# The product x·v and its fold into u on one engine, and another share of evictions, in a long convolution with two MLPs

## The chip, the cores and the metric

The kernel runs on one core of a Trainium2 chip. The metric is the device time of one execution in microseconds, taken as the median of several. A core has TensorE (matrix products), VectorE, ScalarE and GpSimd (elementwise work, each on its own instruction queue) and SP (here it only sends transfers). The trace calls them PE, DVE, ACT, POOL and SP; PEld is TensorE's loading of weights. ScalarE's queue sends transfers too.

## What is computed

A gated long convolution over 12480 positions and 128 channels, then two MLPs of width 2048 in a row:

```python
h_filt = (np.maximum(pos_emb @ w1, 0.0) @ w2) * np.exp(-0.01 * pos)[:, None]
u = x * v
y = irfft(rfft(u, n=2 * S) * rfft(h_filt, n=2 * S), n=2 * S)[:S]
a = x * y
a = np.square(np.maximum(a @ moe_w_in, 0.0)) @ moe_w_out
h = a @ moe2_w_in
out = (h / (1.0 + np.exp(-1.702 * h))) @ moe2_w_out
```

## The kernel before

The convolution is done as products with transform matrices: 12480 positions are laid out as 99 × 127 (with padding), so that a first transform works on 99 partitions and a second one, stage_s2, on the rest. Positions j and -j of the short side are folded into their sum and their difference. The stages follow one another: the filter's hidden layer (filter_stage), the first transform, the second transform with the spectral product and the first half of the inverse (stage_s2), and then one long loop (mlp) that does the last transform and both MLPs tile by tile.

The change lies in the first transform. It has 48 steps of s1_step: 16 over the filter's 64 features (source h, destination G), then 32 over the 128 channels of u (destination A), four columns in each. A step is eight matrix instructions of 99 × 198 (L280) into one of four PSUM banks of the pool cps, and an eviction of that bank, either on VectorE (L284 and L286) or on ScalarE (L288 to L290). Every third step is evicted by VectorE, `f // 4 % 3 == 2`.

u is made beside it, in 16 chunks of eight channels (class Inputs); each chunk serves two of the 32 later steps. load sends x and v of a chunk on SP's queue, in four transfers (L196, L197); chunks 0 to 4 have buffers of their own, the later ones share three (vp), so that load c waits until chunk c-3 has been folded. multiply forms x·v in place on GpSimd, in two halves (L207), and for the even chunks also the sum (even, L215); odd forms the difference on VectorE (L225), and for odd chunks the sum too. u itself has seven buffers, so chunk c needs that the steps of chunk c-7 have been multiplied.

The order is written out by hand (manual_schedule): what is issued first in the code stands first in its engine's queue. advance, called behind each step, issues one multiply, an odd where the step is in the set odds (after steps 1, 4, 6, 9, 11, 13, 16, 18, 21, 23, 25, 28, 30, 33, 35 and 37 of the 48), and then a load if buffers allow. Two more multiplies are issued beside the filter's last two groups. After steps 22, 26, 30 and 34 ScalarE's queue writes a quarter of G to DRAM (gd, L666); stage_s2 reads it back as Gs (load_h, L306), first after step 42. After step 41 the pool of x and v is closed, and w2b (L672) and five loads of matrices m (load_m, L299) are sent on SP in the room that it leaves.

Of the kernel before, what the change touches and what calls it, by code (L numbers as in the profile page):

```python
# [9 lines left out]
FP32 = mybir.dt.float32  # L10
# [4 lines left out]
ALU = mybir.AluOpType  # L15
# [8 lines left out]
N1, N2 = 99, 127  # L24
NT = N1 * N2
JC = N2 // 2
NJ = JC + 1
# [6 lines left out]
XC = 8  # L34
NXC = D // XC
# [5 lines left out]
JF = 8  # L41
# [50 lines left out]
def conv_mlp_kernel(ctx: ExitStack, tc: tile.TileContext, xc, xt, vc, pt, w1, w2,  # L92
                    moe_w_in, moe_w_out, moe2_w_in, moe2_w_out,
                    c_s1, c_s2, c_i2, c_win, out):
    nc = tc.nc
# [84 lines left out]
    class Inputs:  # L180


        def __init__(self, up, pool, first, early):
            self.up, self.pool, self.tiles, self.u = up, pool, {}, {}
            self.first, self.early = first, early
            self.loaded = self.done = self.odd_done = 0

        def load(self):
            c = self.loaded
            if c == NXC or c >= self.early and c - max(self.odd_done, self.early) == 3:  # L190
                return
            self.loaded += 1
            pool, bufs = (self.first, self.early) if c < self.early else (self.pool, 3)
            xs, vs = (pool.tile([N1, XC, 2, NJ], FP32, tag=n, name=n, bufs=bufs) for n in ("x", "v"))
            for r in (slice(0, ROWS), slice(ROWS, N1)):
                nc.sync.dma_start(out=xs[r], in_=xc[c, r])  # L196
                nc.sync.dma_start(out=vs[r], in_=vc[c, r])  # L197
            self.tiles[c] = xs, vs

        def multiply(self):  # L200
            c = self.done
            if c == self.loaded:
                return
            self.done += 1
            xs, vs = self.tiles[c]
            for i in range(0, XC, 4):
                nc.gpsimd.tensor_tensor(out=xs[:, i:i + 4], in0=xs[:, i:i + 4], in1=vs[:, i:i + 4],  # L207
                                        op=ALU.mult)
            self.u[c] = self.up.tile([N1, XC, 2 * NJ], FP32, tag="u", name="u", bufs=7)
            if c % 2 == 0:  # L210
                self.even(c, nc.gpsimd)

        def even(self, c, engine):
            xs, _ = self.tiles[c]
            engine.tensor_tensor(out=self.u[c][:, :, 0:NJ], in0=xs[:, :, 0], in1=xs[:, :, 1], op=ALU.add)  # L215

        def odd(self):
            c = self.odd_done
            if c == self.done:
                return  # L220
            self.odd_done += 1
            if c % 2:
                self.even(c, nc.vector)
            xs, _ = self.tiles.pop(c)
            nc.vector.tensor_tensor(out=self.u[c][:, :, NJ:2 * NJ], in0=xs[:, :, 0], in1=xs[:, :, 1],  # L225
                                    op=ALU.subtract)

    def filter_stage(fp, bank, h, inputs):

        HC = 4  # L230
        NC_ = NJ // HC
        bw1 = fp.tile([128, 128], FP32, name="bw1", bufs=1)
        warm = fp.tile([128, 1], FP32, name="warm", bufs=1)
        win = fp.tile([N1, 2, NJ], FP32, name="win", bufs=1)
        nc.vector.memset(warm, 0.0)
        p_t = {}

        def load_pos(c):
            p = fp.tile([128, HC, N1], FP32, tag="pos", name="pos", bufs=12)
            nc.sync.dma_start(out=p, in_=pt[:, c * HC:(c + 1) * HC, :])  # L240
            p_t[c] = p

        nc.scalar.dma_start(out=bw1, in_=w1)
        for c in range(12):
            load_pos(c)
        nc.scalar.dma_start(out=win, in_=c_win)
        nc.scalar.activation(out=warm, in_=warm, func=ACTF.Sigmoid)
        nc.scalar.dma_start(out=cs1, in_=c_s1)
        nc.vector.memset(sign[:, 0:1], 1.0)
        nc.vector.memset(sign[:, 1:2], -1.0)  # L250

        for j in range(0, NJ, JF):
            for c in range(j // HC + 12, min(j // HC + 12 + JF // HC, NC_)):
                load_pos(c)
            if j >= JF:
                inputs.load()
            ps = bank("hp")[:N1]
            for i in range(JF):
                nc.tensor.matmul(out=ps[:, i * 2 * F:(i + 1) * 2 * F],
                                 lhsT=p_t[(j + i) // HC][:, (j + i) % HC, :], rhs=bw1)  # L260
            r = fp.tile([N1, 2, F, JF], FP32, tag="r", name="r")
            for s in range(2):
                wb = win[:, s, j:j + JF].unsqueeze(1).to_broadcast([N1, F, JF])
                nc.vector.scalar_tensor_tensor(
                    out=r[:, s], in0=ps.rearrange("p (j s f) -> p s f j", j=JF, s=2)[:, s],
                    scalar=0.0, in1=wb, op0=ALU.max, op1=ALU.mult)
            last = j + JF == NJ
            (nc.vector if last else nc.gpsimd).tensor_tensor(
                out=h[:, :, j:j + JF], in0=r[:, 0], in1=r[:, 1], op=ALU.add)
            nc.vector.tensor_tensor(out=h[:, :, NJ + j:NJ + j + JF], in0=r[:, 0], in1=r[:, 1],  # L270
                                    op=ALU.subtract)
            if j >= NJ - 2 * JF:
                inputs.multiply()

    def s1_step(bank, src, d, dst, on_vector):

# [17 lines left out]
    def load_m(mp, p):  # L294
        if p >= NP:
            return
        n = min(2, N1 - 2 * p)
        m_t[p] = mp.tile([128, 2, 2, 128], FP32, tag="m", name="m", bufs=7)
        nc.sync.dma_start(out=m_t[p][:, 0:n], in_=c_s2[:, 2 * p:2 * p + n])  # L299
# [327 lines left out]
    with tc.manual_schedule():  # L627
# [4 lines left out]
        def bank(name):  # L632
            return cps.tile([128, 1024], FP32, tag="b", name=name)
# [1 line left out]
        G = sgs.enter_context(tc.tile_pool(name="G", bufs=1, side="right")).tile(  # L635
            [128, N1, 2, F], FP32, name="G")
        vp = vps.enter_context(tc.tile_pool(name="v", bufs=3, side="right"))
        odds = {-(-12 * c // 5) + 1 for c in range(NXC)}
        steps = [0]

        def advance():
            inputs.multiply()
            if steps[0] in odds:
                inputs.odd()
            inputs.load()
            steps[0] += 1

        with tc.tile_pool(name="h", bufs=1) as hp:
            h = hp.tile([N1, F, 2 * NJ], FP32, name="h")
            inputs = Inputs(up, vp, hp, 5)  # L650
            with tc.tile_pool(name="fil", bufs=2) as fp:
                filter_stage(fp, bank, h, inputs)
            for f in range(0, F, 4):
                s1_step(bank, h, f, G[:, :, :, f:f + 4], f // 4 % 3 == 2)
                advance()
            assert inputs.odd_done >= inputs.early
        with tc.tile_pool(name="A", bufs=1, reuse_waits="tile") as ap_, ExitStack() as mps:
            A = ap_.tile([128, N1, 2, D], FP32, name="A")
            for d in range(0, D, 4):
                s1_step(bank, inputs.u[d // XC], d % XC, A[:, :, :, d:d + 4], d // 4 % 3 == 2)  # L660
                if d // 4 < 25:
                    advance()
                if d // 4 in (6, 10, 14, 18):
                    q = 25 * (d // 16 - 1)
                    q = slice(q, min(q + 25, N1))
                    nc.scalar.dma_start(out=gd[:, q], in_=G[:, q].rearrange("p k c f -> p k (c f)"))  # L666
                if d // 4 == 25:
                    assert inputs.odd_done == NXC
                    vps.close()
                    mp = mps.enter_context(tc.tile_pool(name="mh", bufs=1, reuse_waits="tile"))  # L670
                    w2b = mp.tile([128, 2 * D], FP32, name="w2b")
                    nc.sync.dma_start(out=w2b, in_=w2)  # L672
                if d // 4 in (25, 26, 27, 28, 29):
                    load_m(mp, d // 4 - 25)
                if d // 4 in (26, 28):
                    load_h(mp, (d // 4 - 26) // 2)
            sgs.close()
            ups.close()
            w0 = ctx.enter_context(tc.tile_pool(name="w0", bufs=1, side="right", reuse_waits="tile"))
            split_weights(w0, 0)  # L680
            cp = ctx.enter_context(tc.tile_pool(name="cvt", bufs=1, side="right", reuse_waits="tile"))
            lp = ctx.enter_context(tc.tile_pool(name="lp", bufs=2, side="right", reuse_waits="tile"))
            nc.sync.dma_start(out=ci2, in_=c_i2)
            work = Weights([0, 4, 1, 5, 2, 6], 3, 7, 5, cp, [(44, 3), (46, 7)])
            hooks = {44: [lambda: load_x(lp, 0)]}
            with tc.tile_pool(name="s2", bufs=1, side="right", reuse_waits="tile") as sp:
                stage_s2(sp, mp, A, w2b, hooks, work)
# [91 lines left out]
```

## Time and profile before

| | us |
|---|---|
| median of three runs | 1455.44 (1452.51 to 1455.81) |
| the profiled execution | 1450.28 |
| its span in the trace | 1448.5 |
| TensorE busy | 1410.4 (97%) |
| VectorE busy | 1128.7 (78%) |
| ScalarE busy | 956.9 (66%) |
| GpSimd busy | 278.7 (19%) |

The busy times are of the whole span. A stage may look otherwise than the mean, so the views below are taken by stretch. In a timeline, the bracket at the end of a row says how long the engine had been idle and which instruction's end it waited for.

### The profile page before, as it was taken

What the parts mean: (1) busy time and instruction counts of PE and PEld (TensorE: products, weight loads), DVE (VectorE), ACT (ScalarE), POOL (GpSimd) and SP (SyncE); (2) the same over time, 40 slices, a digit from 0 to 9 for tenths busy, and PEclk for the clock granted to TensorE, in tenths of its full rate; (3) what the DMA queues carried; (4) which work ended last, traced back from release to release, by engine and by line L of the source; (5) the groups of instructions that cost most, each with busy time, mean ns of one, the idle gap of its engine ahead of it and who ended that gap; (6) DMA issues with size and microseconds to landing.
All of it is one profiled execution on the core that took longest, in us unless ns stands there. A gap on an engine that the chain in (4) does not pass through costs nothing.

```text
span 1448.5 us, 17134 instructions
## 1 busy us (share of the span) xinstructions
PE 1410.4 (97%) x6634; PEld 1193.6 (82%) x6634; DVE 1128.7 (78%) x1241; ACT 956.9 (66%) x1117; POOL 278.7 (19%) x249
## 2 busy tenths in 40 slices
PE   7888999999999999999999999999999999999998
PEld 7877888788878888888888888888888888888887
DVE  6736898779987778777777777777787777877887
ACT  1654444376766777767676667777777667777776
POOL 7651222234622100121011210112001120000000
PEclk9999999999999999999999999999999999999999
DMA  9395776522210000100000000000000000000000
GB/s 257 90 299 176 238 245 211 180 81 78 74 37 19 26 26 8 37 19 26 17 18 30 26 26 8 26 30 27 26 8 26 30 26 8 8 8 0 15 15 14
DMA packets 46397, 91.21 MB, mean 63 GB/s; under 512 B 4183, under 2 KB 30604, under 8 KB 45804
## 3 DMA queue, kind: packets, MB, share of 16 engines
q1 hardware_dynamic: 35886, 57.17, 13.5%
q10 hardware_dynamic: 10430, 32.95, 5.9%
q8 instruction: 52, 0.85, 0.2%
q14 instruction: 29, 0.24, 0.1%
HBM read 64.25 MB, written 25.85 MB: 62 GB/s over the span
## 4 chain that ended last, share of the span: by engine, by line
PE 88%; DVE 4%; DMA 4%; issue 2%; ACT 1%; POOL 1%; SPq 0%; POOLq 0%; DVEq 0%; ACTq 0%
PE hin L512 12%; PE hin L511 12%; PE hin L513 12%; PE acc L512 12%; PE acc L511 12%; PE acc L513 12%; PE yps L469 4%; PE s L280 3%; PE hk L339 3%; PE xk L341 3%; PE ob L365 3%; PE fk L328 2%; DMA gd<-G 1%; DVE gl L549 1%; DMA m<-in_c_s_dram 1%
## 5 line engine op out<-in xcount | busy, mean ns | idle before, releaser
L549 DVE TENSOR_TENSOR gl<-g,gh 128x1004 fp32r<-128x1004 f32 (+4 forms) x400 | 491.4, 1229 | 35.1 <-ACT gh L545 34.5
L529 ACT ACTIVATE g<-hin 128x1004 f32<-128x1004 f32 (+4 forms) x200 | 201.2, 1006 | 237.9 <-PE hin L513 237.3
L511 PE MATMUL acc<-gh,w 128*128 128x502 f32 (+4 forms) x800 | 313.5, 392 | 0.4 <-DVE lo L458 0.4
L511 PE MATMUL hin<-hi,w 128*128 128x502 f32 (+4 forms) x800 | 312.7, 391 | 0.0
L512 PE MATMUL acc<-gl,w 128*128 128x502 f32 (+4 forms) x800 | 311.8, 390 | 0.8 <-DVE gl L549 0.8
L512 PE MATMUL hin<-lo,w 128*128 128x502 f32 (+4 forms) x800 | 312.3, 390 | 0.0
L513 PE MATMUL acc<-gh,w 128*128 128x502 f32 (+4 forms) x800 | 311.7, 390 | 0.0
L513 PE MATMUL hin<-hi,w 128*128 128x502 f32 (+4 forms) x800 | 311.5, 389 | 0.0
L416 POOL TENSOR_TENSOR b<-uv 99x256 f32<-99x256 f32 x127 | 159.6, 1286 | 699.0 <-DMA uv<-bd 508.5
L540 DVE TENSOR_TENSOR g<-hin,g 128x1004 f32<-128x1004 f32 (+4 forms) x200 | 238.7, 1193 | 50.6 <-ACT g L532 50.6
L538 DVE CAST gh<-g 128x1004 fp32r<-128x1004 f32 (+4 forms) x200 | 141.6, 708 | 150.8 <-ACT g L530 150.8
L532 ACT ACTIVATE g<-hin 128x1004 f32<-128x1004 f32 (+4 forms) x200 | 200.1, 1000 | 75.2 <-PE hin L513 67.2
L530 ACT ACTIVATE g<-g 128x1004 f32<-128x1004 f32 (+4 forms) x200 | 208.0, 1040 | 6.4
L545 ACT CAST gh<-g 128x1004 fp32r<-128x1004 f32 (+4 forms) x200 | 202.8, 1014 | 0.4 <-DVE g L540 0.4
L511 PEld LDWEIGHTS hin<-hi,w 128*128 128x128 f32 x800 | 151.3, 189 | 33.9 <-ACT g L529 2.4
L512 PEld LDWEIGHTS acc<-gl,w 128*128 128x128 f32 x800 | 151.0, 189 | 31.9 <-DVE gl L549 2.0
L513 PEld LDWEIGHTS hin<-hi,w 128*128 128x128 f32 x800 | 151.3, 189 | 30.7
L511 PEld LDWEIGHTS acc<-gh,w 128*128 128x128 f32 x800 | 151.1, 189 | 31.0 <-DVE lo L458 0.9
L512 PEld LDWEIGHTS hin<-lo,w 128*128 128x128 f32 x800 | 151.3, 189 | 30.6 <-issue 0.5
L513 PEld LDWEIGHTS acc<-gh,w 128*128 128x128 f32 x800 | 150.8, 189 | 30.4
L352 DVE TENSOR_TENSOR t<-xk,hc 128x512 f32<-128x512 f32 (+1 forms) x100 | 63.8, 679 | 25.8 <-PE xk L341 13.9
L469 PEld LDWEIGHTS yps<-ci,b 99*128 99x128 f32 x508 | 62.7, 196 | 8.2 <-issue 2.8
(67 smaller groups left out, 1132.5 us busy)
## 6 DMA issues: line engine op xcount, KB each, us to landing
uv<-bd SPq DMA_DIRECT2D x64, 198.0 KB
m<-in_c_s_dram SPq DMA_DIRECT2D x49, 256.0 KB
bd<-bs ACTq DMA_DIRECT2D x24, 512.0 KB
x<-in_xc_dram SPq DMA_DIRECT2D x16, 384.0 KB
v<-in_vc_dram SPq DMA_DIRECT2D x16, 384.0 KB
Gs<-gd ACTq DMA_DIRECT2D x12, 512.0 KB
gd<-G ACTq DMA_DIRECT2D x3, 1600.0 KB
raw<-in_moe_w_in_dram SPq DMA_DIRECT2D x8, 512.0 KB
```

The source lines that it names most:

```text
L416: engine.tensor_tensor(out=b[:, :, s, c], in0=uv[:, 0, :, c], in1=uv[:, 1, :, 1 - c], op=ALU.add if s != c else ALU.subtract)
L469: nc.tensor.matmul(out=ps[:, o:o + w], lhsT=b[:, c, :], rhs=ci2[:, c, r:r + w], start=(c == 0), stop=(c == 1))
L511: nc.tensor.matmul(out=out, lhsT=a, rhs=hl[0], start=first, stop=False)
L512: nc.tensor.matmul(out=out, lhsT=a, rhs=hl[1], start=False, stop=False)
L513: nc.tensor.matmul(out=out, lhsT=b, rhs=hl[0], start=False, stop=last)
L529: nc.scalar.activation(out=g, in_=ps, func=ACTF.Relu)
L530: nc.scalar.activation(out=g, in_=g, func=ACTF.Square)
L532: nc.scalar.activation(out=g, in_=ps, func=ACTF.Sigmoid, scale=1.702)
L538: nc.vector.tensor_copy(out=gh, in_=g)
L540: nc.vector.tensor_tensor(out=g, in0=ps, in1=g, op=ALU.mult)
L545: nc.scalar.copy(out=gh, in_=g)
L549: nc.vector.tensor_tensor(out=gl, in0=g, in1=gh.bitcast(FP32), op=ALU.subtract)
```

## The change

The product, the sum and the difference of a chunk become one fold, three instructions on VectorE, and GpSimd has no part in it any more. Folds are issued after steps 1, 4, 6, 8, 10, 12, 15, 18, 20, 22, 24, 26, 28, 30, 32 and 34. Of nine steps VectorE evicts two (the fourth and the eighth, counted anew for u), ScalarE the other seven: 10 and 38 of the 48, where it was 15 and 33. The two products beside the filter's last groups are gone. The pool of x and v is closed three steps earlier, after step 38, and the five loads of m follow from there, while the first read-back of G stays behind step 42.

```diff
         def load(self):
             c = self.loaded
-            if c == NXC or c >= self.early and c - max(self.odd_done, self.early) == 3:
+            if c == NXC or c >= self.early and c - max(self.done, self.early) == 3:
                 return
...
-        def multiply(self):
+        def fold(self):
             c = self.done
             if c == self.loaded:
                 return
             self.done += 1
-            xs, vs = self.tiles[c]
-            for i in range(0, XC, 4):
-                nc.gpsimd.tensor_tensor(out=xs[:, i:i + 4], in0=xs[:, i:i + 4], in1=vs[:, i:i + 4],
-                                        op=ALU.mult)
-            self.u[c] = self.up.tile([N1, XC, 2 * NJ], FP32, tag="u", name="u", bufs=7)
-            if c % 2 == 0:
-                self.even(c, nc.gpsimd)
-
-        def even(self, c, engine):
-            xs, _ = self.tiles[c]
-            engine.tensor_tensor(out=self.u[c][:, :, 0:NJ], in0=xs[:, :, 0], in1=xs[:, :, 1], op=ALU.add)
-
-        def odd(self):
-            c = self.odd_done
-            if c == self.done:
-                return
-            self.odd_done += 1
-            if c % 2:
-                self.even(c, nc.vector)
-            xs, _ = self.tiles.pop(c)
-            nc.vector.tensor_tensor(out=self.u[c][:, :, NJ:2 * NJ], in0=xs[:, :, 0], in1=xs[:, :, 1],
+            xs, vs = self.tiles.pop(c)
+            u = self.u[c] = self.up.tile([N1, XC, 2 * NJ], FP32, tag="u", name="u", bufs=7)
+            nc.vector.tensor_tensor(out=xs, in0=xs, in1=vs, op=ALU.mult)
+            nc.vector.tensor_tensor(out=u[:, :, 0:NJ], in0=xs[:, :, 0], in1=xs[:, :, 1], op=ALU.add)
+            nc.vector.tensor_tensor(out=u[:, :, NJ:2 * NJ], in0=xs[:, :, 0], in1=xs[:, :, 1],
                                     op=ALU.subtract)
...
-            if j >= NJ - 2 * JF:
-                inputs.multiply()
...
-        odds = {-(-12 * c // 5) + 1 for c in range(NXC)}
+        folds = {max(-(-11 * c // 5) + 1, 2 * c + 4 if c >= 7 else 0) for c in range(NXC)}
         steps = [0]
 
         def advance():
-            inputs.multiply()
-            if steps[0] in odds:
-                inputs.odd()
+            if steps[0] in folds:
+                inputs.fold()
             inputs.load()
             steps[0] += 1
...
-                s1_step(bank, h, f, G[:, :, :, f:f + 4], f // 4 % 3 == 2)
+                s1_step(bank, h, f, G[:, :, :, f:f + 4], f // 4 % 9 in (3, 7))
                 advance()
...
-                s1_step(bank, inputs.u[d // XC], d % XC, A[:, :, :, d:d + 4], d // 4 % 3 == 2)
-                if d // 4 < 25:
+                s1_step(bank, inputs.u[d // XC], d % XC, A[:, :, :, d:d + 4], d // 4 % 9 in (3, 7))
+                if d // 4 < 22:
                     advance()
...
-                if d // 4 == 25:
-                    assert inputs.odd_done == NXC
+                if d // 4 == 22:
+                    assert inputs.done == NXC
                     vps.close()
                     mp = mps.enter_context(tc.tile_pool(name="mh", bufs=1, reuse_waits="tile"))
                     w2b = mp.tile([128, 2 * D], FP32, name="w2b")
                     nc.sync.dma_start(out=w2b, in_=w2)
-                if d // 4 in (25, 26, 27, 28, 29):
-                    load_m(mp, d // 4 - 25)
+                if 22 <= d // 4 < 27:
+                    load_m(mp, d // 4 - 22)
```

## Rows read from the trace of the kernel before

**Rows 1.** The page's first line.
```profile
span 1448.5 us, 17134 instructions
```

**Rows 2.** Windows: stretch, its length, each engine's busy us (instructions), clock, DMA share, GB/s.
```profile
25.80:121.00 95.20, 79.24 (x385) 75.18 (x385) 53.54 (x54) 55.95 (x99) 52.64 (x38) 0.86 0.66 208
121.00:275.00 154.00, 151.05 (x791) 134.90 (x792) 130.07 (x199) 74.41 (x129) 43.51 (x50) 1.00 0.64 212
275.00:1448.50 1173.50, 1164.01 (x5333) 967.67 (x5331) 926.98 (x960) 825.10 (x887) 166.37 (x148) 0.99 0.08 27
```

**Rows 3.** Timeline of ScalarE, evictions (L288 is the first instruction of three).
```profile
34.24 0.81 ACT L288 COPY G<-s 64x792 f32<-64x792 f32 x1 [1.06 <-PE s L280]
...
35.98 0.81 ACT L288 COPY G<-s 64x792 f32<-64x792 f32 x1
...
68.38 0.81 ACT L288 COPY A<-s 64x792 f32<-64x792 f32 x1 [0.58 <-PE s L280]
...
72.40 0.81 ACT L288 COPY A<-s 64x792 f32<-64x792 f32 x1 [0.58 <-PE s L280]
...
110.73 0.81 ACT L288 COPY A<-s 64x792 f32<-64x792 f32 x1 [5.67 <-DVE u L225]
```

**Rows 4.** Timeline of TensorE: start, duration, line, operation, tiles, count, [idle before, releaser].
```profile
25.82 17.77 PE L280 MATMUL s<-cs,h 99*128 99x198 f32 x88 [5.98 <-DVE h L270]
...
86.11 10.41 PE L280 MATMUL s<-cs,u 99*128 99x198 f32 x40 [3.65 <-DVE A L286]
...
107.49 1.58 PE L280 MATMUL s<-cs,u 99*128 99x198 f32 x8 [0.76 <-DVE A L286]
112.31 6.49 PE L280 MATMUL s<-cs,u 99*128 99x198 f32 x24 [3.25 <-DVE A L286]
120.98 1.16 PE L328 MATMUL fk<-m,Gs 128*128 128x128 f32 x8 [2.17 <-ACT A L290]
```

**Rows 5.** Windows again, the four us after TensorE's pause.
```profile
86.00:90.00 4.00, 3.89 (x12) 3.89 (x13) 0.05 (x1) 0.00 (x0) 1.65 (x2) 0.51 0.97 243
```

**Rows 6.** Timeline of VectorE: filter (L268, L270), folds (L225), evictions (L284, L286).
```profile
20.42 0.69 DVE L270 TENSOR_TENSOR h<-r 99x512 f32<-99x512 f32 x1
...
22.35 1.66 DVE L268 TENSOR_TENSOR h<-r 99x512 f32<-99x512 f32 x1
23.92 1.75 DVE L270 TENSOR_TENSOR h<-r 99x512 f32<-99x512 f32 x1
...
71.18 0.69 DVE L225 TENSOR_TENSOR u<-x 99x512 f32<-99x512 f32 x1
71.89 0.97 DVE L284 COPY A<-s 64x792 f32<-64x792 f32 x1
72.88 0.98 DVE L286 TENSOR_TENSOR A<-s,sign 64x792 f32<-64x792 f32 x1
...
109.57 0.69 DVE L225 TENSOR_TENSOR u<-x 99x512 f32<-99x512 f32 x1
```

**Rows 7.** Groups by line and form, VectorE: count, busy us, mean ns, idle before.
```profile
L549 DVE TENSOR_TENSOR gl<-g,gh 128x1004 fp32r<-128x1004 f32 x176 | 219.1, 1245 | 19.7 <-ACT gh L545 19.3
```

**Rows 8.** Timeline of SP, first of the four transfers of loads 8 and 10.
```profile
52.23 0.32 SPq L196 DMA_DIRECT2D x<-in_xc_dram  x1
...
67.99 0.32 SPq L196 DMA_DIRECT2D x<-in_xc_dram  x1
```

**Rows 9.** Timeline of GpSimd, the product that needs load 8.
```profile
58.22 2.49 POOL L207 TENSOR_TENSOR x<-x,v 99x512 f32<-99x512 f32 x2 [6.60 <-DMA v<-in_vc_dram]
```

**Rows 10.** DMA queues (q1 SP, q10 ScalarE): packets, MB, share; 52 to 58.5, then 72 to 100.
```profile
q1 hardware_dynamic: 236, 0.81, 44.0%
...
q10 hardware_dynamic: 560, 6.28, 57.1%
q1 hardware_dynamic: 1025, 3.54, 43.0%
```

**Rows 11.** Waits of SP's queue, 0 to 130 us: total, times, longest.
```profile
SPq L197 <- DMA gd<-G: 10.3, 2, 8.1
```

More of the change, by code (lines that the diff above doesn't have):

```diff
@@ L185, in __init__ @@
             self.first, self.early = first, early
-            self.loaded = self.done = self.odd_done = 0
+            self.loaded = self.done = 0
         def load(self):
             c = self.loaded
-            if c == NXC or c >= self.early and c - max(self.odd_done, self.early) == 3:
+            if c == NXC or c >= self.early and c - max(self.done, self.early) == 3:
                 return
@@ L653, in conv_mlp_kernel @@
             for f in range(0, F, 4):
-                s1_step(bank, h, f, G[:, :, :, f:f + 4], f // 4 % 3 == 2)
+                s1_step(bank, h, f, G[:, :, :, f:f + 4], f // 4 % 9 in (3, 7))
                 advance()
-            assert inputs.odd_done >= inputs.early
+            assert inputs.done >= inputs.early
         with tc.tile_pool(name="A", bufs=1, reuse_waits="tile") as ap_, ExitStack() as mps:
```

## Prediction

> **What bounds the kernel now.** I read the windows first. The span is 1448.5 us [rows 1]; the execution that left the trace took 1450.28 us, 0.35% below the median of the three runs, 1455.44. In the second transform (121 to 275 us) and in the MLP (from 275 us) TensorE is busy 151.05 of 154.0 and 1164.01 of 1173.5 us at a clock of 1.00 and 0.99 [rows 2]: the change touches neither, and nothing of them gets shorter. In the first transform (25.8 to 121) TensorE is busy 79.24 of 95.2 us at a mean clock of 0.86, and no other engine is busy more than 56 us [rows 2]. So no engine is the bound there; waits are.
>
> I number its 48 steps s0 to s47: s0 to s15 work on the filter, s16 to s47 on u, two steps for each of the 16 chunks. Where ScalarE's eviction follows a wait for TensorE, steps 22 and 25 become ready at 68.38 and 72.40 [rows 3]: three steps in 4.02 us, so 1.34 us for one at full clock and 64.3 us for 48. The stretch takes 95. The loss stands in the timeline of TensorE: it sits idle for 3.65 us before 86.11 and for 3.25 us before 112.31, both times for an eviction by VectorE [rows 4], and after the first of these the granted clock is 0.51, the lower of its two levels (1.2 GHz of 2.4) [rows 5]; the last three steps take 6.49 us, 2.16 each [rows 4]. These evictions were late because VectorE takes its work in order and a fold stood in front, which waited for GpSimd's product, which waited for a load.
>
> **The fold moves to VectorE.** Removed: 32 products and 8 sums on GpSimd, 8 sums and 16 differences on VectorE. Added: 16 times a product over 1024 elements, a sum and a difference over 512, all on VectorE. The sum and the difference take 0.69 us where GpSimd rests, and up to 1.75 where it works on x and v [rows 6]; from s0 on GpSimd will have nothing. The product over 1024 isn't in the trace: the nearest row is 1.245 us for 1004 elements of the same type, both inputs in SBUF [rows 7], so 1.27. It can't be below the 0.69 of half the size, nor, were 1.75 for 512 VectorE's own pace, above 3.5; I take 1.27, since 0.69 is what the row shows with GpSimd at rest. The next instruction follows a fold after 0.71 (71.18 to 71.89, [rows 6]). One fold is 1.27 + 0.69 + 0.69 = 2.65 us; bounds 2.07 and 7.0, of which the upper has no cause once GpSimd is empty and stays out of the range. That is 42.4 us on VectorE.
>
> **The evictions.** One costs VectorE 0.97 + 0.98 and two gaps, 2.0 us [rows 6], and ScalarE 1.74 us (34.24 to 35.98, [rows 3]). VectorE keeps 10 of 15, ScalarE has 38 instead of 33: 66 us of work in a stretch that won't fall below 80. Seven of nine is 1.35 us a step, at TensorE's own 1.34, hidden as long as VectorE or the loads are slower. VectorE's total is 42.4 + 20 = 62 us; per nine steps 4.5 folds and two evictions make 15.9 us, 1.77 us a step. So VectorE paces the steps while it folds, with TensorE some 75% busy.
>
> **The start.** Two products no longer run on GpSimd beside the filter's last group. Its two last VectorE instructions took 1.66 and 1.75 us [rows 6]; with 0.69 each (20.42, the same instruction alone) they end at 22.35 + 1.4 = 23.75 instead of 25.67, and s0 starts 2.0 us earlier, at 23.8 instead of 25.82 [rows 4]. s3, behind which ScalarE waited, was done at 34.22 [rows 3] and is at 32.2.
>
> **Until the ninth fold.** The first eviction of VectorE is now that of s3. From there to the end of fold 9 VectorE has 4 evictions (s3, s7, s12, s19) and 9 folds (1 to 9; fold 0 lies in front): 8.0 + 23.9 = 31.9, ending at 64.1. Loads 8 and 9 are sent when folds 5 and 6 are done, at about 51.5 and 54.1, and a load without company is there 6.0 us after its issue (52.23 to 58.22, [rows 8, 9]), before VectorE comes to it. Today fold 9 ends at 71.18 + 0.69 = 71.87 [rows 6]. Gained so far: 7.8 us.
>
> **From there the loads.** Chunks 5 to 15 share three pairs of buffers: load c leaves when fold c-3 is done. Fold c now comes six steps behind fold c-3 instead of seven, and today's four writes of G to DRAM, issued from ScalarE's queue after s22, s26, s30 and s34, fall into the same time. Prices: load 8 alone used 44.0% of 6.5 us of all 16 DMA engines, 2.9 us; the writes used 57.1% of 28 us, 16.0 us [rows 10], 4 us each. VectorE alone would end fold 15 at 32.2 + 7 × 2.0 + 15 × 2.65 = 86. The DMA engines have 16 + 5 × 2.9 = 30.5 us of work from the first write on, at about 61 (s22 ends at 32.2 + 19 × 1.34 = 57.7 at the earliest, and is evicted after s20 and s21): 91.5, and with fold 15 behind it 94.2, the lower end. The upper end is today's own stretch from fold 9 to fold 15, 71.87 to 110.26, 38.4 us [rows 6]: 64.1 + 38.4 = 102.5. Of that stretch one load goes, since load 10 now leaves at 56.8, ahead of the writes (it left at 67.99, [rows 8]), 2.9 us; and product, sum and difference of the last one cost 2.65 instead of 2.49 on GpSimd [rows 9] and up to 1.4 on VectorE, 1.2 us less. I take 38.4 - 4.1 = 34.3, fold 15 ending at 98.4, nearer to what was measured than to the ideal sum.
>
> In the stretch from 72 to 100 us the writes hold 57.1% and the loads 43.0% of the DMA engines' time [rows 10], and the queue that sends the loads stands still behind a write for 8.1 us at once [rows 11]. The Trainium skill (DMA: Bandwidth & Descriptors, section Queues, rings and completion order) says that a DMA engine takes turns between queues at the bounds of packets; by that rule a queue with large packets (560 for 6.28 MB here) holds back one with small ones (1025 for 3.54 MB), which speaks against earlier loads beside the same writes. By even shares the five loads would be over after twice 14.5 us, at 90, and fold 15 at 92.7; by the row they are over last, which is the sum above.
>
> **The tail.** From the end of fold 15 (110.26) to the first matmul of the next stage (120.98, [rows 4]) 10.7 us pass: one or two late evictions, then three steps at 2.16. ScalarE too stood still then, 5.67 us at the read-back of G, which needs the buffers that fold 15 frees [rows 3]. In the changed kernel fold 15 comes after s34 instead of s37, with the evictions of s37, s41 and s46 left to VectorE. At best 8.7 us (two steps at the faster clock), at worst the case below; I keep 10.7. The next stage's loads (five of matrices, which move from after s41..s45 to after s38..s42 on SP, and two of G) also wait for fold 15, as today, and 10.7 us carried them.
>
> **Sum.** 98.4 + 10.7 = 109.1 instead of 120.98: 11.9 us. 1450.28 - 11.9 = 1438.4 for such an execution, and 1455.44 - 11.9 = 1443.5 at the level of the median, which I predict.
>
> **Rivals.** (a) The DMA stretch is as long as today: fold 15 at 102.5, next stage at 113.2, gain 7.8, 1447.6. For it: the same bytes, in the stretch that is at its limit. Against: load 10 leaves it. (b) The loads don't hold VectorE up: fold 15 at 86, the next stage at 96.7, gain 24, 1431. Against it: 30.5 us of DMA work have no room. (c) TensorE can't run past a held eviction: after fold 15 VectorE evicts s37 (2.0 us), and if s41 needs that bank, seven steps at 2.16 and an eviction follow, 2.0 + 15.1 + 1.7 = 18.8 instead of 10.7; the next stage at 117.2, gain 3.8, 1451.6, no change that shows. For it: four banks; against: today s44 ran at 107.49 (the three last steps follow at 112.31, [rows 4]), with the eviction of s39 still queued behind fold 15, which ended at 110.26. (d) Slower: SP stands still behind a write of G at each of the four, 8.1 us each, 32.4 instead of 10.3 us in all [rows 11]; load, fold and the evictions behind it on VectorE are late by 22 us, fold 15 ends at 120.5, gain -10.2, 1465.6. It takes the gain away from 22.2 us of such waits on, and is slower by 0.3% from 26.6. For it: the loads now have one step less; against: loads 8 to 11 leave before the first write or with it.
>
> **How the numbers follow.** A measurement of this kernel can tell 0.3%, 4.4 us, from no change. Chances: the forecast (gain 9 to 18) 0.5; (a) 0.22; (b) 0.06; (c) 0.12; (d) 0.1. Faster is the forecast with (a) and (b), 0.78; same (c), 0.12; slower (d), 0.1. The forecast's own range is 94.2 + 8.7 to 102.5 + 10.7: 1437.4 to 1447.6. To hold 8 in 10 the range takes in (a) and most of (c), and on the lower side a little towards (b): 1435 to 1453.
>
> **What would show it.** s0 starting at 23.8; products of 1.27 and sums of 0.69 on VectorE with GpSimd empty; fold 9 ending near 64; SP waiting for VectorE and hardly for G; fold 15 near 98 and the next stage near 109, with the rest of the trace shifted as it is. Wrong would be: folds of over 3 us, TensorE at 0.5 through long parts of the stretch, SP behind writes for over 20 us, or a second transform that gets longer than 154 us.

## The result

| | before | forecast | after |
|---|---|---|---|
| median, us | 1453.97 (4 runs; 1455.44 in the three shown above) | 1443.5 | 1436.40 (1435.51 to 1442.02) |
| the profiled execution | 1450.28 | 1438.4 | 1442.02 |
| s0 starts | 25.82 | 23.8 | 24.74 |
| fold 9 ends | 71.87 | 64.1 | 64.30 |
| fold 15 ends | 110.26 | 98.4 | 101.30 |
| the next stage starts | 120.98 | 109.1 | 110.97 |

After is faster: the ratio of its time to that of before is 0.989, with a 95% interval of 0.9857 to 0.9924, so 11 to 21 us. The same kernel run once more gave 0.9905 (0.9869 to 0.994). The traces show 10.0 us of gain up to the next stage (120.98 - 110.97), 11.0 in the second run.

The windows of after, in the stretches of [rows 2] (length, busy us of PE, PEld, DVE, ACT and POOL with instructions, clock, DMA share, GB/s):

```profile
24.74:110.97 86.23, 75.93 (x384) 70.46 (x385) 59.29 (x68) 63.47 (x112) 0.00 (x0) 0.91 0.75 233
110.97:265.00 154.03, 151.42 (x791) 135.09 (x792) 129.35 (x199) 75.08 (x132) 43.76 (x50) 1.00 0.64 213
265.00:1440.20 1175.20, 1165.56 (x5333) 969.05 (x5331) 928.92 (x960) 825.08 (x887) 165.18 (x148) 0.99 0.08 27
```

The first transform is 9 us shorter and its clock rose from 0.86 to 0.91; GpSimd does nothing in it; the rest is as it was. TensorE's timeline, which answers [rows 4], and VectorE's, which answers [rows 6]:

```profile
24.74 24.30 PE L262 MATMUL s<-cs,h 99*128 99x198 f32 x128 [3.87 <-DVE h L254]
...
80.72 7.31 PE L262 MATMUL s<-cs,u 99*128 99x198 f32 x32 [3.58 <-ACT A L272]
...
103.36 6.84 PE L262 MATMUL s<-cs,u 99*128 99x198 f32 x24 [3.14 <-DVE A L268]
110.97 1.13 PE L310 MATMUL fk<-m,Gs 128*128 128x128 f32 x8 [0.77 <-PE s L262]
```

```profile
23.30 0.69 DVE L252 TENSOR_TENSOR h<-r 99x512 f32<-99x512 f32 x1
23.91 0.68 DVE L254 TENSOR_TENSOR h<-r 99x512 f32<-99x512 f32 x1
24.51 1.22 DVE L207 TENSOR_TENSOR x<-x,v 99x1024 f32<-99x1024 f32 x1
...
63.62 0.68 DVE L209 TENSOR_TENSOR u<-x 99x512 f32<-99x512 f32 x1
64.33 0.97 DVE L266 COPY A<-s 64x792 f32<-64x792 f32 x1
...
93.60 1.22 DVE L207 TENSOR_TENSOR x<-x,v 99x1024 f32<-99x1024 f32 x1 [8.05 <-DMA v<-in_vc_dram]
...
100.62 0.68 DVE L209 TENSOR_TENSOR u<-x 99x512 f32<-99x512 f32 x1
```

The filter's last two instructions take 0.69 and 0.68 instead of 1.66 and 1.75; the product (L207) takes 1.22. TensorE runs 24.30 us without a pause from s0 on, where it had 17.77 before. Up to fold 9, which ends at 63.62 + 0.68 = 64.30, all goes nearly as forecast. After it VectorE stands 8.05 us before the fold of chunk 14, for a load. The reason is in the timeline of SP, in that of ScalarE, and in the waits of all up to 130 us (total, times, longest):

```profile
91.25 0.25 SPq L196 DMA_DIRECT2D x<-in_xc_dram  x1
```

```profile
68.57 0.36 ACTq L647 DMA_DIRECT2D gd<-G  x1
78.59 0.33 ACTq L647 DMA_DIRECT2D gd<-G  x1
78.96 0.81 ACT L270 COPY A<-s 64x792 f32<-64x792 f32 x1 [4.82 <-DMA gd<-G]
86.16 0.33 ACTq L647 DMA_DIRECT2D gd<-G  x1
86.53 0.81 ACT L270 COPY A<-s 64x792 f32<-64x792 f32 x1 [1.56 <-DMA gd<-G]
```

```profile
SPq L196 <- DMA gd<-G: 15.9, 1, 15.9
DVE x L207 <- DMA v<-in_vc_dram: 15.9, 5, 8.0
ACT A L270 <- DMA gd<-G: 6.4, 2, 4.8
```

The third of the four transfers of load 14 stands on SP's queue for 15.9 us and leaves at 91.25, behind the fourth write of G. The third and fourth writes themselves stand on ScalarE's queue until the one before is over, and ScalarE's evictions stand behind them, 6.4 us, which is what TensorE waits for at 80.72. In before SP's wait behind G was 10.3 us [rows 11], and ScalarE had none. That SP waits for a write which has not even left is no matter of bandwidth: SP comes to this transfer at 75.3, the fourth write leaves at 86.16. The list of waits in the built program (not a view of the trace) tells why. Each transfer of SP's and ScalarE's queues signals its end on one of eight semaphores, which are handed out in turn in the order that the program was planned in, and waits first for the transfer that had its semaphore before it. In before the writes stand seven, six and seven places apart in that order and have four different semaphores. In after they stand exactly eight apart and have one; and eight places behind the fourth write stands the third transfer of load 14.

### The profile page after: what moved, and what is told of

The parts are those of the page before. It is cut to its first block, busy times and chain, and to the rows that moved or that the text cites. A ratio compares the mean times of both kernels' runs of the same rounds, so it can differ in the third digit from the quotient of the medians.

```text
span 1440.2 us, 17101 instructions
## 1 busy us (share of the span) xinstructions
PE 1409.9 (98%) x6634; PEld 1191.4 (83%) x6634; DVE 1133.7 (79%) x1255; ACT 965.1 (67%) x1132; POOL 221.6 (15%) x209
## 4 chain that ended last, share of the span: by engine, by line
PE 87%; DMA 5%; DVE 4%; ACT 1%; issue 1%; POOL 0%; SPq 0%; DVEq 0%; POOLq 0%; ACTq 0%
PE hin L494 12%; PE hin L493 12%; PE hin L495 12%; PE acc L494 12%; PE acc L493 12%; PE acc L495 12%; PE yps L451 4%; PE hk L321 3%; PE ob L347 3%; PE xk L323 3%; PE s L262 2%; DMA gd<-G 2%; PE fk L310 2%; DMA v<-in_vc_dram 1%; DVE gl L531 1%
## 5 line engine op out<-in xcount | busy, mean ns | idle before, releaser
L338 POOL TENSOR_TENSOR P<-t,t 128x256 f32<-128x256 f32 (+1 forms) x50 | 43.8, 875 | 197.7 <-DVE t L334 94.6
```

## The experiments

All times are in us; the marks are from the trace of each run. "Third fk" is the start of the third group of matrix instructions of the next stage (L310), which is a steadier mark than the first where that stage starts with pauses. An edit can also change two things that the builder hands out anew for each kernel: the turn of the semaphores, and which of the four PSUM banks a step gets. Where that bears on a reading it is said.

| run | median | ratio to before (95%) | s0 | fold 9 | fold 15 | next stage | third fk |
|---|---|---|---|---|---|---|---|
| before | 1450.4 to 1454.0 | | 25.82 | 71.9 | 110.3 | 120.98 | 128.99 |
| after | 1436.40 | 0.989 (0.9857 to 0.9924) | 24.74 | 64.3 | 101.3 | 110.97 | 118.95 |
| after_again | 1437.14 | 0.9905 (0.9869 to 0.994) | 24.33 | 63.9 | 100.2 | 109.99 | 117.97 |
| fold_only | 1445.23 | 0.9968 (0.9949 to 0.9988) | 23.30 | 75.9 | 105.4 | 118.14 | 126.66 |
| evict_only | 1440.06 | 0.9924 (0.9896 to 0.9951) | 25.83 | 67.8 | 102.4 | 107.26 | 120.12 |
| contend | 1445.82 | 0.997 (0.995 to 0.999) | 25.74 | 79.6 | 110.7 | 118.80 | 127.27 |
| gd_pool | 1434.57 | 0.9894 (0.9868 to 0.9921) | 24.31 | 71.4 | 98.0 | 105.82 | 114.57 |
| gd_gated | 1431.38 | 0.9855 (0.9835 to 0.9874) | 23.51 | 62.4 | 90.8 | 100.94 | 112.56 |
| half_gdpool | 1428.44 | 0.9821 (0.9788 to 0.9854) | 24.24 | 65.6 | 90.4 | 100.11 | 108.10 |
| fold_gdpool | 1457.10 | 1.0039 (1.0024 to 1.0054) | 24.49 | 74.6 | 101.8 | 130.65 | 139.77 |
| gd_apart | 1440.31 | 0.9916 (0.9895 to 0.9937) | 24.12 | 75.6 | 102.6 | 112.44 | 120.55 |
| gated_late | 1428.21 | 0.984 (0.9809 to 0.9871) | 23.86 | 62.5 | 90.6 | 101.15 | 109.90 |

**after_again: the changed kernel once more.**

> The changed kernel once more, for a second profile: its first profiled execution took 1442.0 us, its other three 1435.5 to 1437.3. Theory 1 (from the end of fold 9 on the DMA engines have some 30 us of work and set the pace): the gain in time before the second transform starts is 10 us in every profile, and the next stage starts near 111 us as in the first. Theory 2 (the pace there is set by queues that stand still until a particular write of G has ended, which differs from run to run): in this profile SP's wait behind writes of G, 15.9 us in the first, is a different one, and the start of the second transform moves with it, to 104 to 111 us. Time 1435 to 1442 by both.

SP's wait behind G was again 15.9 us and ScalarE's 6.3; fold 15 ended at 100.2. So these waits are not an accident of one execution: they belong to the program's order.

**fold_only: product and fold on VectorE, evictions as before.**

```diff
-                s1_step(bank, h, f, G[:, :, :, f:f + 4], f // 4 % 9 in (3, 7))
+                s1_step(bank, h, f, G[:, :, :, f:f + 4], f // 4 % 3 == 2)
```

(and the same for u.)

> The product and the fold on VectorE as in the changed kernel, but VectorE evicts every third step as before (15 evictions instead of 10). Theory: VectorE has 5 x 2.0 = 10 us more to do, 7 evictions instead of 4 until fold 9, which so ends at 70 instead of 64.3 us; it paces 1.99 us a step instead of 1.77. Time 1441 to 1448, so the folds alone bring a half or less. Rival (the loads set the end, VectorE has slack): the same 1436 to 1438 as with both parts.

1445.23, some 5 us below before. Two things go against each other here. The start is early (23.30), and fold 8 ends at 61.8; then VectorE waits 9.6 us for load 9, since SP stands 12.1 and 7.3 us behind writes of G. The time lies in the theory's range, but fold 9 ends at 75.9 and not at 70. The number is that of the folds with another distribution of the semaphores and another order of the banks (see evict_only), not of the folds alone.

**evict_only: before, with the new share of evictions.**

```diff
-                s1_step(bank, h, f, G[:, :, :, f:f + 4], f // 4 % 3 == 2)
+                s1_step(bank, h, f, G[:, :, :, f:f + 4], f // 4 % 9 in (3, 7))
```

(and the same for u.)

> The kernel before with seven of nine evictions on ScalarE, and product and folds as they were. Theory: VectorE's evictions were late because of what stood in front of them (folds that wait for GpSimd), and there still is; five of them moved away save a part of it, 2 to 6 us: 1448 to 1453. Rival (the gain lies in the shared evictions, not in the fold): 1436 to 1441.

1440.06: the rival had the time right and my theory had it wrong. This kernel is some 10 us faster than before, twice the gain of fold_only. GpSimd works as in before and s0 starts as in before (25.83), but fold 9 ends 4 us earlier, fold 15 8 us, and the stretch from fold 15 to the next stage is 4.9 us instead of 10.7. In TensorE's timeline of this kernel:

```profile
90.07 14.16 PE L280 MATMUL s<-cs,u 99*128 99x198 f32 x64 [6.66 <-DVE A L286]
104.47 2.95 PE L280 MATMUL s<-cs,u 99*128 99x198 f32 x16 [0.24 <-DVE A L286]
107.26 1.06 PE L328 MATMUL fk<-m,Gs 128*128 128x128 f32 x8
```

There is one long wait for an eviction by VectorE (6.66 us) instead of the two before 86.11 and 112.31 [rows 4], and behind fold 15 only one of 0.24. But all of TensorE's waits for VectorE's evictions in this stage are 6.9 us here and 8.4 in before, so that fewer evictions stand in VectorE's line behind a fold that waits explains little of the gain. Something else is gone as well, which before's timeline has:

```profile
49.18 1.61 PE L280 MATMUL s<-cs,h 99*128 99x198 f32 x8 [1.80 <-ACT G L290]
52.59 5.65 PE L280 MATMUL s<-cs,h 99*128 99x198 f32 x16 [1.80 <-ACT G L290]
```

Twice TensorE stands 1.80 us, the length of one eviction, for ScalarE's eviction of the step that it has just done. In the built program of before three steps in a row (s12 to s14) have the same bank; in evict_only no two have, and in its trace there is no such pause. TensorE's waits for ScalarE's evictions of G, 4.1 us in before, are gone, and fold 9 ends 4.1 us earlier. So this run changes the share of the evictions, the order of the banks and the turn of the semaphores (SP stands 9.3 us behind G, in one wait, instead of 10.3 in two), and what each of them is worth is not shown. Part of the early start is lost at once: the third group of fk is 8.9 us earlier than in before, not 13.7.

**contend: after, with company on GpSimd.** The kernel adds work: 32 products of a constant tile on GpSimd, two at each fold, that nothing uses or waits for.

```diff
...
+            for i in range(2):
+                nc.gpsimd.tensor_tensor(out=busy, in0=busy, in1=busy, op=ALU.mult)
             nc.vector.tensor_tensor(out=xs, in0=xs, in1=vs, op=ALU.mult)
...
```

> The changed kernel with 32 products of 99 x 512 on GpSimd added, of a constant tile by itself in place, on which nothing waits: as many as the kernel before had there. They run from about 22 to 65 us. This prices GpSimd's company alone, without the wait of a fold for its product. Theory 1 (VectorE's operations with two SBUF inputs are slowed by GpSimd, 0.69 to 1.75 us): folds of 4 to 6 us until 65, fold 7 at 65 to 75 instead of 56.6, the second transform 6 to 12 us later, 1443 to 1449. Theory 2 (the chain load, product, fold was the cost, the company not): 1436 to 1439.

1445.82, some 9 us more than after and in the range of theory 1; the order of the banks is that of after. The groups of VectorE's instructions between 24 and 70 us (busy, mean ns), first of this kernel, then of after:

```profile
L210 DVE TENSOR_TENSOR x<-x,v 99x1024 f32<-99x1024 f32 x8 | 14.0, 1753 | 0.1
L211 DVE TENSOR_TENSOR u<-x 99x512 f32<-99x512 f32 x8 | 11.2, 1402 | 0.3
L212 DVE TENSOR_TENSOR u<-x 99x512 f32<-99x512 f32 x7 | 10.7, 1523 | 0.0
```

```profile
L207 DVE TENSOR_TENSOR x<-x,v 99x1024 f32<-99x1024 f32 x11 | 13.4, 1222 | 0.6 <-DMA v<-in_vc_dram 0.5
L208 DVE TENSOR_TENSOR u<-x 99x512 f32<-99x512 f32 x11 | 7.6, 691 | 0.5
L209 DVE TENSOR_TENSOR u<-x 99x512 f32<-99x512 f32 x11 | 7.5, 683 | 0.0
```

A fold costs 1.75 + 1.40 + 1.52 = 4.68 us beside GpSimd and 1.22 + 0.69 + 0.68 = 2.60 without it, and fold 9 ends 15.3 us later. The price of the fold in the forecast, 2.65, holds because GpSimd is empty, as it said.

**gd_pool: after, with the writes of G on GpSimd's queue.**

```diff
-                    nc.scalar.dma_start(out=gd[:, q], in_=G[:, q].rearrange("p k c f -> p k (c f)"))
+                    nc.gpsimd.dma_start(out=gd[:, q], in_=G[:, q].rearrange("p k c f -> p k (c f)"))
```

> The changed kernel, but the four writes of G to DRAM are sent from GpSimd's queue, which is empty in this stage, instead of ScalarE's; the same bytes at the same place in the order of the code. Theory 1 (DMA work sets the pace from fold 9 on): the same bytes take the same time, 1434 to 1438. Theory 2 (the queues that stand still behind a write set it: SP 15.9 us at once, ScalarE 8 us in three waits of its evictions): neither can wait for a write of G any more, loads 14 and 15 leave some 10 us earlier, the second transform starts at 100 to 104 instead of 111 us: 1424 to 1430.

No load shares a semaphore with a write now, and SP and ScalarE have no wait behind G. But GpSimd has nothing in front of the writes:

```profile
51.52 2.31 POOL L647 DMA_DIRECT2D gd<-G  x4 [28.76 <-ACT G L272]
```

All four leave at 51.5, ahead of loads 9 and 10, for which VectorE waits 7.8 and 3.5 us; fold 9 is 7 us late, and from fold 12 on VectorE waits for no load. 1434.57 lies within the spread of after's two series (1432.57 to 1442.02), though in the trace the third fk is 4.4 us earlier: one hindrance was mostly traded for another. (In after ScalarE stood 6.4 us in two waits, not the 8 in three of the text above.)

**gd_gated: the same, each write held until a fold is done** (8, 10, 12 and 14).

```diff
...
-                if d // 4 in (6, 10, 14, 18):
+                if d // 4 in (4, 8, 12, 16):
...
+                    nc.gpsimd.tensor_copy(out=gate, in_=inputs.u[inputs.done - 1][0:1, 0, 0:1])
                     nc.gpsimd.dma_start(out=gd[:, q], in_=G[:, q].rearrange("p k c f -> p k (c f)"))
```

> As gd_pool (the writes of G go out from GpSimd's queue), but each write is held until fold 8, 10, 12 and 14 is done, by a copy of one element of that fold's u on GpSimd ahead of it. With gd_pool all four left at 51.5 to 53.8 us and held up loads 9 to 11 (VectorE waited 7.8 and 3.5 us for them). Theory (what counts is that loads come ahead of writes; the DMA engines then have room): fold 9 ends at 64 again, fold 15 at 86 to 92 instead of 98.0, the second transform starts at 98 to 102 instead of 105.8; 1426 to 1431. Rival (the DMA engines' total work sets the end, in whatever order): fold 15 at 96 to 99, 1433 to 1436.

This tells the cause of the long stretch. The writes leave at 59.05, 66.97, 76.21 and 86.36, within 2.4 us of after's (59.66, 68.57, 78.59, 86.16), the bytes are the same, and so is the order on VectorE; but nobody stands behind a write. Fold 15 ends at 90.8 instead of 101.3. Of these 10.5 us 1.9 are there at fold 9 already (62.4 instead of 64.3); the stretch from fold 9 to fold 15 is 28.4 us instead of 37.0. The windows of it, first of after, then of this kernel, and VectorE's waits for loads in the first transform:

```profile
64.30:101.30 37.00, 30.02 (x152) 26.36 (x150) 20.98 (x24) 23.38 (x42) 0.00 (x0) 0.95 0.78 269
62.39:90.79 28.40, 24.60 (x122) 21.25 (x121) 20.99 (x24) 20.23 (x37) 2.97 (x6) 0.94 0.99 359
DVE x L208 <- DMA v<-in_vc_dram: 7.4, 4, 2.9
```

VectorE is busy 21 us in both and waits for nothing but loads: 7.4 us instead of 15.9, and these 8.5 us are nearly all of the difference of 8.6. They are the price of the waits behind writes. The DMA engines are busy 0.99 of the shorter stretch and 0.78 of the longer one, 28.1 and 28.9 us: without the waits their work is what fills it. 1431.38; the next stage starts at 100.94, but its third group 112.56 is only 6.4 earlier than in after.

**half_gdpool: gd_pool without the loads of v from chunk 5 on.** The kernel leaves out part of the work: from chunk 5 on v isn't loaded, and x·x takes the place of x·v.

```diff
...
-                nc.sync.dma_start(out=vs[r], in_=vc[c, r])
+                if c < self.early:
+                    nc.sync.dma_start(out=vs[r], in_=vc[c, r])
...
-            nc.vector.tensor_tensor(out=xs, in0=xs, in1=vs, op=ALU.mult)
+            nc.vector.tensor_tensor(out=xs, in0=xs, in1=vs if c < self.early else xs, op=ALU.mult)
...
```

> gd_pool with v not loaded from chunk 5 on; the product there is x times x, so u is another number from chunk 5 on, while all instructions on VectorE stay. Loads 5 to 15 move half the bytes. Theory 1 (loads hold the folds up from fold 8 on): no wait of VectorE for a load, fold 15 at 85 to 89 as VectorE's own sum (86) says, the second transform at 95 to 99; 1423 to 1428. Theory 2 (something else paces it, the loads only show it): fold 15 at 95 to 98 as in gd_pool; 1432 to 1435.

Fold 15 at 90.4, 7.6 earlier than in gd_pool, between the two theories: VectorE still waits 6.5 us for x beside the writes that leave together. Half of the loads' bytes are worth as much as the gates of gd_gated, which moves them all.

**fold_gdpool: fold_only with the writes on GpSimd's queue.** The edit is that of gd_pool, made to fold_only.

> fold_only (product and fold on VectorE, every third step evicted by VectorE) with the writes of G sent from GpSimd's queue. In fold_only SP stood behind writes of G for 19.4 us (15.9 in the changed kernel). Theory 1 (VectorE's five evictions more cost it 10 us of its own time, whatever the transfers do): fold 15 at 101 to 104, the tail 12 us, second transform at 113 to 116; 1440 to 1444. Theory 2 (fold_only was held by the waits behind writes): 1434 to 1437, as gd_pool.

Slower than before, by the stretch that I had held fixed, and neither theory had it. SP has no wait behind G, and fold 15 ends at 101.8, 3.6 earlier than in fold_only; but the next stage starts 28.9 us after it. The windows of this kernel:

```profile
80.00:90.00 10.00, 6.41 (x19) 5.35 (x18) 8.62 (x11) 3.39 (x6) 0.00 (x0) 0.50 0.91 228
90.00:100.00 10.00, 6.41 (x23) 5.57 (x23) 9.73 (x12) 3.39 (x6) 0.00 (x0) 0.67 0.49 129
100.00:110.00 10.00, 8.20 (x25) 7.68 (x24) 3.70 (x5) 3.04 (x6) 0.00 (x0) 0.50 0.65 217
```

From 80 to 100 VectorE is busy 18.4 of 20 us: it makes up the folds that load 9 held up, with every third eviction in line behind them, while ScalarE is busy 6.8. But it is not VectorE that TensorE waits for. Here are two of TensorE's rows, one eviction by ScalarE, and TensorE's waits for all of them:

```profile
82.51 3.01 PE L262 MATMUL s<-cs,u 99*128 99x198 f32 x8 [1.80 <-ACT A L272]
87.31 4.84 PE L262 MATMUL s<-cs,u 99*128 99x198 f32 x16 [1.80 <-ACT A L272]
```

```profile
85.55 0.81 ACT L270 COPY A<-s 64x792 f32<-64x792 f32 x1 [3.10 <-PE s L262]
...
86.76 0.49 ACT L272 ACTIVATE A<-s 64x396 f32<-64x396 f32 x1
```

```profile
PE s L262 <- ACT A L272: 17.5, 12, 1.8
```

The step that ends at 85.52 is evicted by 87.25, and only then, at 87.31, does TensorE begin the next one. There are nine such pauses of 1.80, and no wait for an eviction by VectorE; in the built program these nine steps have the bank of the step just before them (two in before, none in after, four in fold_only, one in gd_pool; each has that many pauses of 1.80 in its trace). The granted clock is 0.50 to 0.67 meanwhile, mostly the lower of its two levels. When fold 15 is done, ten steps have not begun (three in after); they take 1.96 to 2.63 us each, with three of the pauses between them. gd_pool, with the new share of evictions and another order of banks, takes 22.5 us less. So the run shows what it costs when steps must follow one another through a single bank; it does not price the share of the evictions.

**gd_apart: after, with three transfers of 4 bytes on ScalarE's queue** that move on the turn of the semaphores, so that the four writes have four different ones.

```diff
...
+                if d // 4 in (8, 12, 16):
+                    e = d // 16
+                    nc.scalar.dma_start(out=tiny[:, e:e + 1], in_=c_s1[0:1, e:e + 1])
                 if d // 4 in (6, 10, 14, 18):
```

> The changed kernel, with three transfers of 4 bytes added on ScalarE's queue, after steps 24, 28 and 32 of the first transform. They carry no data that is used; they only move on the turn in which completion semaphores are handed out, so that by the program's listing the four writes of G signal on four different semaphores (1, 2, 3, 4) instead of all on the same one. Theory: in the changed kernel ScalarE stood 6.4 us in two waits behind a write of G, and SP 15.9 us in one, because a transfer that signals on a semaphore waits for the one before it on the same. Then here the third and the fourth write leave while an earlier one is still running, ScalarE stands behind writes of G for less than 1 us in all, and SP's one wait of 15.9 us is gone (each later load can still meet the semaphore of a write, by a few us). Fold 15 ends at 95 to 99 instead of 101.3, the next stage starts at 105 to 109 instead of 111, and the time is 1431 to 1436. Rival: the writes of one queue go one after another in any case; then the waits at the third and fourth write stay at 4 to 6 us in all, writes leave at the end of the previous one, and the time is the changed kernel's 1435 to 1439.

The first half came as the theory said, the second did not. ScalarE has no wait behind G any more: the writes leave at 58.11, 64.08, 72.63 and 83.41, the third 6.0 us earlier than in after. The waits of SP moved to other loads and grew (total, times, longest):

```profile
SPq L197 <- DMA gd<-G: 19.5, 3, 11.8
SPq L198 <- DMA gd<-G: 2.7, 1, 2.7
```

22.2 us instead of 15.9, now first at load 9: VectorE stands 13.35 us for it, fold 9 ends at 75.6, and fold 15 at 102.6, no earlier than in after. So the semaphores decide who stands. Four different ones for the writes are not enough, as long as the loads take their turn at the same eight.

**gated_late: gd_gated, with the second read-back of G issued after s47 instead of s44.**

```diff
-                if d // 4 in (26, 28):
-                    load_h(mp, (d // 4 - 26) // 2)
+                if d // 4 in (26, 31):
+                    load_h(mp, (d // 4 - 26) // 5)
```

> The kernel with writes of G from GpSimd's queue, each held until a fold is done, with one edit: the second read-back of G on ScalarE's queue is issued after the last step of the first transform (s47) instead of after s44. In the run without this edit ScalarE stood 1.75 us at that issue with two evictions of the transform queued behind it, the last one ended at 104.06, and the copy that the second transform's first products wait for came only at 104.09. Theory: that wait sets the start of the second transform; then the last eviction ends at 102.3, the third group of fk starts at 110.5 to 111.2 instead of 112.56, and the time is 1429 to 1431 instead of 1431.4. Rival: the second half of G is then late for the second group of fk, which waits for it; the third group starts at 112.5 to 114.5 and the time is 1431 to 1434.

The next stage now runs on from its start with shorter pauses than in gd_gated (4.4 us from the first group of fk to the second, where it was 6.2):

```profile
101.15 1.06 PE L311 MATMUL fk<-m,Gs 128*128 128x128 f32 x8
103.72 1.13 PE L322 MATMUL hk<-w2b,fs 128*128 128x256 f32 x4 [1.51 <-ACT fs L314]
...
105.55 1.05 PE L311 MATMUL fk<-m,Gs 128*128 128x128 f32 x8
```

The third group starts at 109.90, 2.7 us earlier than in gd_gated and a little earlier than the theory had it, although the start of the stage, which the theory wanted earlier, did not move (101.15 and 100.94). 1428.21 is the lowest time of a kernel that does all the work, some 8 us below after, though the intervals of the two overlap a little; from gd_gated's 1431.38 the times alone do not tell it apart.

## Why the prediction came out as it did

The direction was right, and 1436.4 lies in the range, near its lower end. The mechanism held up to fold 9. The stretch behind it was sized by a row that showed a wait on a semaphore and not the shares of the DMA engines. And one thing that the forecast had no term for, the order of the banks, keeps the experiments from dividing the gain between folds and evictions. By the steps:

**The start**, 2.0 us: 1.1 (24.74), 1.5 in the second run. The filter's two instructions did drop to 0.69 and 0.68, but its last group itself came 0.9 later than in the sum. That is within what runs with the same code in this place show (23.30 to 24.74).

**The price of a fold**, 2.65: 1.22 + 0.69 + 0.68 and the gaps, 2.65 from the product at 61.68 to the eviction at 64.33. The nearest row [rows 7] was the right one; contend shows what the reason "GpSimd is empty" is worth.

**Fold 9** at 64.1: 64.30. The chain of 4 evictions and 9 folds was the right count. It began at 33.00 instead of 32.2 and took 31.3 us instead of 31.9: that the two differences nearly cancel is luck.

**The evictions** were booked as hidden on ScalarE, and as 10 us less on VectorE. In after TensorE waits 5.0 us in all for ScalarE's evictions, 3.58 of them while ScalarE stands behind a write, so that the hiding held nearly. That they alone would bring little, which I expected of evict_only, was wrong: it is 10.4 us faster than before. How much of that is theirs stays open. Before loses 3.6 us in two pauses that come from the order of the banks and that after and evict_only don't have, and fold_gdpool is slow by nine of them; the forecast followed VectorE's line and never asked which bank a step gets. The gains of fold_only and evict_only, 5.2 and 10.4 us, add up to more than the 13.3 of both edits in the same comparison, and no run makes one of the two edits with banks and semaphores held as they were.

**The stretch from fold 9 to fold 15**, 34.3: 37.0 (64.30 to 101.30), above my value and below the bound of 38.4. I took all of it for the DMA engines' work, and that was the wrong step: 8.5 us of it are waits behind writes (gd_gated). In gated_late, with all bytes, the stretch is 28.1 us (62.5 to 90.6), somewhat below the lower end of the forecast, 30.1 (64.1 to 94.2), which was the sum of the DMA engines' work; that sum was nearly right, and choosing a value nearer to before's own stretch took in a wait that has another cause. SP's 8.1 us [rows 11], like its 15.9 in after, were a wait on a semaphore, and I had used that row as if it spoke of the shares of two queues in the DMA engines. The Trainium skill (DMA: Bandwidth & Descriptors, section Queues, rings and completion order) has a DMA engine take turns between queues at the bounds of packets. No run here shows these turns. Even shares, which the forecast set beside that rule and which gave 92.7, come nearer than my reading where nobody stands behind a write and the writes are spread (90.8 in gd_gated, 90.6 in gated_late), but not in gd_pool, where all four leave at once (98.0).

**Rivals (a) and (b)**: the stretch lies 1.4 us below (a)'s 38.4, and in after the loads do hold VectorE up, against (b), by 15.9 us in five waits; without the shared semaphore (gated_late) it is 6.9 in four, and fold 15 comes 4.6 us behind (b)'s 86.

**Rival (d)**, SP behind each write, came in part: 15.9 us in one wait, where the text expected SP to wait "hardly for G", and with ScalarE behind writes as well, which I had not thought of. Its price was too high: at 22.2 us of such waits the gain was to be gone, but gd_apart has 22.2 and its third group of fk is still 8.4 us earlier than before. A wait of SP is not passed on whole: in after its 15.9 us became 8.05 of VectorE's at that load.

**The tail**, 10.7: 9.7, with one pause of 3.14 and three steps in 6.84, as forecast. But it is no constant: 4.9 in evict_only, 28.9 in fold_gdpool. It goes with the steps that TensorE has left, its pauses and its clock: three steps, one pause and a clock of 0.65 in after, three and a half steps with a pause of 0.24 at a clock of 1.00 in evict_only, ten steps with three pauses at 0.65 in fold_gdpool. The lower end of 8.7 was not what its reason gives: two steps of 1.34 instead of 2.16 save 1.6, so 9.1. Rival (c) did not come in after: there was one pause of 3.14 and no second.

**The whole**: 11.9 forecast. -0.2 up to fold 9, -2.7 in the stretch of the loads, +1.0 in the tail; and behind the next stage's start the trace of after is 1.7 longer than that of before (1329.2 against 1327.5), which makes 8.3 by the spans (1448.5 - 1440.2). That 1.7 isn't given back by the change: behind the third group of fk the rest takes 1319.5 in before and 1314.3 to 1321.3 in the other eleven traces, in after 1321.3 and in its second run 1318.3. The profiled execution of after is also the slowest of its four, by 4.8 us. So the median fell by 17.6 (13.3 in the second comparison, 1450.47 to 1437.14), and I had put it on the level of the first three runs of before, the highest median of before seen. The traces account for 10 to 11 us, a little less than the forecast; that the median came out 7 us below the 1443.5 lies in the spread of the executions, is not settled, and is no merit of the forecast.

## What to carry to other kernels

Before a stall in a transfer queue is priced as bandwidth, look up what the transfer waits for: in a program with few completion semaphores a small load can stand behind a large write of another queue, and an edit that changes the number or the order of the transfers between them can move that wait somewhere else. Large transfers that are not urgent belong where the urgent ones share nothing with them, and they should be held until the urgent ones are out. Before two runs that differ by one edit are subtracted, compare what the builder handed out anew in each, the semaphores of the transfers and the banks of the steps: a pause as long as one eviction, right behind the step that is evicted, is the mark of two steps in a row on one bank.

## What the runs showed of the hardware that was not expected

- A transfer of 12 KB on one queue stood 15.9 us for a write of 1.5 MB on another, because it has the same semaphore; with the writes on GpSimd's queue, at times within 2.4 us of the old ones, nothing stood, and the stretch from fold 9 to fold 15 took 28.4 us instead of 37.0.
- GpSimd's products on a tile that VectorE never touches make VectorE's sums of 512 elements 1.40 and 1.52 us instead of 0.69 and 0.68, and its product of 1024 elements 1.75 instead of 1.22.
- In fold_gdpool TensorE's granted clock was 0.50 to 0.67 in the three stretches shown, mostly the lower of the two levels, and the steps behind fold 15 took 1.96 to 2.63 us instead of 1.34. There TensorE stood 1.80 us after every one to three steps, and the pauses came with slower steps as well.
